# Loading two small inputs of a recurrent layer two tokens per partition, and turning them by products on quarters of the array

## The chip, the core and the metric

The kernel runs on one core of a Trainium2 chip. Its engines each work through a list of instructions of their own: TensorE (PE, matrix products; PEld are its weight loads), VectorE (DVE), ScalarE (ACT), GpSimd (POOL) and SyncE (SP), which here only issues transfers. SBUF is the on-chip memory with 128 partitions, PSUM the memory of 8 banks that TensorE writes, DRAM the memory outside. The metric is the time of one execution on the device in microseconds (us); lower is better.

## The reference

A recurrent attention layer (RWKV-7) over 4 batch elements, 8 heads, 768 tokens and 40 dimensions per head, followed by a feed-forward layer with a squared ReLU:

```python
for t in range(S):
    y[:, :, t] = np.einsum('bhd,bhde->bhe', rt, state)
    Sa = np.einsum('bhde,bhe->bhd', state, at)
    state_decay = state * wt[:, :, None, :] - np.einsum('bhd,bhe->bhde', Sa, bt)
    state = state_decay + np.einsum('bhd,bhe->bhde', vt, kt)
...
x = np.ascontiguousarray(attn_out.transpose(0, 2, 1, 3)).reshape(B * S, H * D)
...
h = np.maximum(x @ w_in, 0.0)
return (h * h @ w_out).astype(np.float32)
```

`r`, `k`, `v`, `w`, `a` and `b` have the shape (4, 8, 768, 40), `w_in` (320, 2048) and `w_out` (2048, 320). What matters for the change: every one of the six inputs has to be brought into SBUF and, but for parts of their use, turned so that the 40 dimensions of a head lie along the partitions and the tokens along the columns.

## The kernel before

The tokens are cut into 24 chunks of 128 tokens of one batch element (`order`). A chunk `i` has an early part, which doesn't depend on the state, and a late part, which does.

The early part (`early`, six steps, written e`i`.1 to e`i`.6 in the order below) loads `w`, `b` and `a` as 128 tokens in 128 partitions by 8 heads of 64 columns, 40 of them used (`fetch`, L146; the buffers are `in_w`, `in_ab` and, for chunks 0 and 1, `in_b`). It turns `w` by four transposes (`turn`, L331), makes the running products of the decays by scans on DVE (L372 to L381, into the tile `decay`, or `dec` for chunks 0 and 1), turns `b` and `a` by four transposes each, multiplies them with the decays (L387, L388), forms products of `a` and `b` within the chunk, and copies them from PSUM into the tile `N` on ScalarE (L401 to L403). Parts of `N` go to DRAM (`kept_q`, `kept_m`, `kept_n`, `kept_d`), and so does the tile of decays (`kept_e`). GpSimd takes the small triangular systems up from there and solves them (L483, L485), in eleven units of 1 to 4 chunks, and stores the result in `kept_t`.

The late part loads `dec` from `kept_e`, `k`, `r`, `v` and `b`, and the solved blocks (`blocks` from `kept_t`, joined to larger inverses by products of 32x32 in `inverses`, tiles `spares`, `T`). It turns `k`, `r` and `v`, and runs `chain`: it begins two banks of `x` from the state, solves for the corrections with `T` and `N` (copies into `apart_x` and `minus_x` on ScalarE in between), updates the state and leaves the tokens of the output in `tokens`. `Ffn` then computes the feed-forward layer on pairs of chunks: `thirds` and `whole` make the hidden units, `square` squares them on ScalarE, and `make_quarter` makes a quarter of the sum over `w_out`. The tokens of a pair are first moved between partitions by eight small transfers (`gather`, L746).

The order of work is written out by hand, in two ways. Up to about 345 us (the opening) it is a list of words: `e3.4` is step 4 of the early part of chunk 3, `LA4` loads `b` and `a` of chunk 4, `lr1` and `lv2` load `r` of chunk 1 and `v` of chunk 2, `sN2` and `sE2` store chunk 2's `N` and decays, `rv1` turns `r` and `v` of chunk 1, `x0` and `c0` are steps of chunk 0's chain, `B1` loads blocks, `J1` joins them, `W1` loads feed-forward weights, `pa` and `pd` round them, `f10` is ten filling products that write nothing of use. An `@a` or `@g` puts a word's transfers on ScalarE's or GpSimd's queue in place of SyncE's. From chunk 7 on it is a fixed slot for each chunk (`sorted_slot`), in which chunk `i` is finished, chunk `i+1` is prepared, and in slots 7 to 13 the early parts of chunks 14 to 23 are done (two each in slots 7 to 9, one each after that). Stores in a slot are put off by one or two places (`store`, `later`, L110). At a slot's end `loads` issues the transfers of the chunk after next.

PSUM is dealt out from three rotating pools: `ps_w` with four banks, `ps_c` with two, `ps_f` with two.

Of the kernel before, what the change touches and what calls it, by code (L numbers as in the profile page):

```python
# [17 lines left out]
def kernel(  # L18
# [73 lines left out]
    def new(name, shape, bufs):  # L92
        return work.tile(shape, FP32, tag=name, name=name, bufs=bufs)
# [37 lines left out]
    for nm, n, fill in (("w", 2, 1.0), ("ab", 4, 0.0), ("b", 2, 0.0)):  # L131
        rings[nm] = Ring(f"in_{nm}", n, [128, H, DP], fill, pads)

# [14 lines left out]

    def load_early(i):
        early_loaded[i] = {nm: fetch(ring, src, i) for nm, ring, src in (("w", "w", w), ("b", "b" if i < 2 else "ab", b), ("a", "ab", a))}  # L150
        if i < 2:
            loaded[i] = {"b": early_loaded[i]["b"]}

# [142 lines left out]
    def as_they_are():  # L296
# [4 lines left out]
        for f in range(NF):  # L301
# [7 lines left out]
    kept_n = [dram.tile([2, HC, NP, HC], FP32, tag=f"n{i}", name=f"kept_n{i}") for i in range(len(order))]  # L309
# [16 lines left out]
                        tag=f"t{u}", name=f"kept_t{u}") for u, (_, nb) in enumerate(units)]  # L326

# [32 lines left out]
    def early(i, g=None, apart=False):  # L360
# [14 lines left out]
        if not apart:  # L375
            bT_, aT_ = turn(x_["b"]), turn(x_["a"])
# [6 lines left out]
        if apart:  # L383
            bT_, aT_ = turn(x_["b"]), turn(x_["a"])
            yield
# [3 lines left out]
        if opened:  # L389
            waiting["e", i] = lambda: on_queue[0].dma_start(out=kept_e[i], in_=dec[:USED])  # L390
        else:
            store(kept_e[i], dec[:USED], 2)
        yield
        bb, c = order[i]
        t_ = new("N", [128, 2, H, HC], 1)


        for e, p_ in enumerate(products(bT, aT[:, :, :C])):
            for group in range(2):
                own_, qs = slice(group * HC, (group + 1) * HC), slice(2 * group, 2 * group + 2)  # L400
                nc.scalar.copy(t_[own_, group, e:NP:2], p_[:HC, qs, :HC])  # L401
                nc.scalar.copy(t_[own_, group, NP + e::2], p_[HC:, qs, HC:])  # L402
            nc.scalar.copy(t_[:HC, 1, e::2], p_[:HC, :, HC:])  # L403
# [14 lines left out]
        if g is None:  # L418
            between = t_[:HC, 1].rearrange("s (w b j) t -> s w b j t", w=2, b=2)
            for e in range(2):  # L420
                moved.append((kept_n[i][e].rearrange("s (w j) t -> s w (j t)", w=2), between[:, :, e].rearrange("s w j t -> s w (j t)"), nc.sync))
# [5 lines left out]
        if g is not None:  # L427
            g["N"] = new("N21", [C, NP, HC], 2)
            for e in range(2):
                nc.scalar.copy(g["N"][e * HC:(e + 1) * HC].rearrange("s (w j) t -> s w j t", w=2),  # L430
                               t_[:HC, 1].rearrange("s (w b j) t -> s w b j t", w=2, b=2)[:, :, e])
            g["joins"] = spare("joins", i)
            for half in range(2):
                nc.scalar.copy(g["joins"][half * HC:half * HC + Q], joins(half))
# [61 lines left out]
    def arrive(i, g, queue=nc.sync):  # L496
        if "N" not in g:
            g["N"] = new("N21", [C, NP, HC], 2)
            queue.dma_start(out=g["N"], in_=kept_n[i].rearrange("b s q t -> (b s) q t"))
# [138 lines left out]
    def chain(i, g):  # L638
# [4 lines left out]
        x_ = [psum(pool)[:, :DM // 2].rearrange("t (h d) -> t h d", d=D) for pool in (ps_w, ps_c)]  # L643
# [266 lines left out]
    fourth = [(n, min(n + 3, NF // 2), flat(t_)) for n, t_ in zip(range(0, NF // 2, 3), rings["ab"].tiles)]  # L910
# [85 lines left out]
    def load_ab(m_):  # L996
        early_loaded.setdefault(m_, {}).update({nm: fetch("ab", src, m_) for nm, src in (("b", b), ("a", a))})
# [87 lines left out]
    def loads(j):  # L1085
        if j < len(order):
            n = ready.setdefault(j, {})
            n["dec"] = kept_here[j % 2]
            nc.sync.dma_start(out=n["dec"][:USED], in_=kept_e[j])
            fetch_next(j, "k", "b")  # L1090
            if not soon(j) and unit_of[j] < FINE:
                arrive(j, n)
            if soon(j) and j > B:
                n["joining"] = inverses(j, n)
                next(n["joining"], None)
# [8 lines left out]
    def sorted_slot(i, g, ch):  # L1104
# [26 lines left out]
        elif more:  # L1131
            begin(j, n)
        step(second.make_quarter)
        if fine and not early_join:
            join()
        step(of(turn_rv), at_place)
        fetch_next(j + 1, "r")
        sums(1)
        step(second.make_quarter, at_place)
        solved_ahead = i > LAID  # L1140
        step(*[on(ch)] * (not solved_ahead), of(decay_state), at_place)
        sums(0)
        sums(2)
# [8 lines left out]
        if not early_join and not fine:  # L1152
            join()
        step(*[on(ch)] * (not solved_ahead), at_place)
        step(at_place, of(turn_k))
        step(of(turn_down), at_place)
        if fine:
            join()
        step(at_place, on(ch))
# [75 lines left out]
```

## Time and profile before

| | |
|---|---|
| time, median of 3 runs (lowest, highest) | 952.38 us (950.92, 957.40) |
| the profiled execution: its time, its span | 956.81 us, 955.1 us |
| mean granted clock of TensorE | 0.945 |
| ScalarE waiting for a turned `r` (L565), in total and longest | 62.8 us, 14.4 us |
| SyncE issues of `in_ab`, median (longest) | 0.67 us (5.98) for `b`, 0.76 us (2.42) for `a` |
| transposes of `in_ab`, from the first to the last | 6.5 to 585.0 us |

The times of rows are microseconds from the start of the span, and the profiled execution is one of several. A group's line in the profile names the engine, the line of the code, the tile written and the tiles read; `128*64 128x80` means 128 rows and 64 columns of weights and 128 by 80 moving elements. A float32 product stands in the trace as two MATMUL rows, a transpose as one. In an order of time, the figure in brackets is how long the engine had been idle and what released it. `SPq` is SyncE's issue of a transfer, `DMA` a transfer that someone waited for.

### The profile page before, as it was taken

The page shows a single profiled execution, that of the slowest core. Times are in us where ns is not written, and L with a number is a line of the kernel's source. Part 1 is how long each engine was busy: PE and PEld are TensorE (multiplying, and loading weights), DVE is VectorE, ACT ScalarE, POOL GpSimd, SP SyncE. Part 2 cuts the span into 40 slices and gives each one's busy share as a digit, 9 for nine tenths or more (in the row PEclk, how much of TensorE's full clock was granted, in tenths as well). Part 3 has the DMA queues.
Part 4 walks back from the last instruction along what each step waited for, and adds up shares of the span by engine and source line. Part 5 has one row for each costly group of instructions (what it writes and reads, how often), then busy time and mean ns, then how long its engine had stood idle before and what let it go on. Part 6 is the DMA issues. An engine that isn't in the chain of part 4 may idle for free.

```text
span 955.1 us, 22646 instructions
## 1 busy us (share of the span) xinstructions
PE 867.8 (91%) x9004; PEld 722.9 (76%) x9004; DVE 444.3 (47%) x1127; ACT 370.0 (39%) x965; POOL 463.0 (48%) x871
## 2 busy tenths in 40 slices
PE   6467888788899999997998999999999999999998
PEld 4345556567777778777787788798899998888897
DVE  5914764888573325543525336443364333333022
ACT  4040535534635254353442553443423333422321
POOL 4557318147003876772059994879999700000000
PEclk9766996878999999998999999999999999999999
DMA  9749858956676567886868644752345443240000
GB/s 106 128 111 146 155 125 164 209 149 121 155 133 143 111 114 160 153 136 125 140 128 133 102 89 80 133 128 49 67 73 93 93 90 66 36 79 1 22 14 14
DMA packets 260338, 102.05 MB, mean 107 GB/s; under 512 B 235594, under 2 KB 249930, under 8 KB 259210
## 3 DMA queue, kind: packets, MB, share of 16 engines
q1 hardware_dynamic: 251493, 83.00, 48.8%
q0 software_dynamic: 3840, 15.79, 6.7%
q10 hardware_dynamic: 4901, 1.83, 0.9%
q8 instruction: 71, 1.16, 0.6%
q14 instruction: 33, 0.27, 0.1%
HBM read 67.82 MB, written 30.79 MB: 103 GB/s over the span
## 4 chain that ended last, share of the span: by engine, by line
PE 67%; DMA 9%; DVE 9%; ACT 7%; SPq 5%; issue 3%; POOL 0%; DVEq 0%; ACTq 0%; POOLq 0%
PE ps_f L87 33%; PE ps_w L87 18%; PE ps_c L87 8%; PE ps_w L331 4%; DMA dec<-kept_e 2%; SPq L110 2%; DMA in_r<-in_r_dram 2%; PE ps_c L691 1%; ACT hid L802 1%; SPq L746 1%; DMA in_w<-in_w_dram 1%; ACT N L402 1%; PE ps_f L264 1%; ACT N L401 1%; PE ps_c L603 1%
## 5 line engine op out<-in xcount | busy, mean ns | idle before, releaser
L485 POOL TENSOR_TENSOR half_t<-half_t,half_p 128x126 f32<-128x126 f32 (+43 forms) x374 | 216.0, 578 | 29.3
L483 POOL TENSOR_TENSOR half_p<-half_n,half_t 128x126 f32<-128x126 f32 (+43 forms) x374 | 196.6, 526 | 63.2 <-DMA half_n<-kept_q 25.8
L87 PE MATMUL ps_f<-tokens,w_in 128*128 128x256 f32 x672 | 157.6, 388 | 0.0
L87 PE MATMUL ps_f<-w_out,hid 128*128 128x160 f32 (+1 forms) x736 | 153.1, 361 | 0.3 <-ACT hid L802 0.3
L87 PEld LDWEIGHTS ps_f<-tokens,w_in 128*128 128x128 f32 x672 | 126.4, 193 | 24.3 <-issue 8.0
L87 PEld LDWEIGHTS ps_f<-w_out,hid 128*128 128x128 f32 x736 | 116.7, 191 | 23.9 <-issue 1.8
L794 ACT ACTIVATE hid<-ps_f 128x512 f32<-128x512 f32 x84 | 49.0, 595 | 110.7 <-PE ps_f L87 109.9
L401 ACT COPY N<-ps_w 64x128 f32<-64x128 f32 x96 | 24.8, 258 | 104.4 <-PE ps_w L87 88.3
L723 DVE TENSOR_TENSOR state<-ps_w,state 40x160 f32<-40x160 f32 x40 | 12.9, 321 | 98.0 <-PE ps_w L87 97.7
L456 POOL DMA_DIRECT2D half_n<-kept_q x20 | 10.5, 529 | 95.9 <-DMA kept_m<-N 32.0
L802 ACT ACTIVATE hid<-hid 128x512 f32<-128x512 f32 x96 | 56.3, 625 | 0.5
L347 DVE TENSOR_TENSOR RX<-ps_w,upper 128x512 f32<-128x512 f32 x48 | 30.9, 685 | 50.1 <-PE ps_w L87 50.1
L372 DVE TENSOR_TENSOR_SCAN decay<-ps_w,ones 128x64 f32<-128x64 f32 x88 | 23.7, 270 | 65.0 <-PE ps_w L331 65.0
L264 PE MATMUL ps_f<-ident 128*128 128x512 f32 (+3 forms) x108 | 50.5, 603 | 0.0
L87 PE MATMUL ps_f<-tokens,w_third 64*128 64x256 f32 x336 | 46.7, 390 | 0.1
L739 DVE TENSOR_TENSOR tokens<-ps_c,dec 128x512 f32<-128x512 f32 x24 | 16.6, 692 | 62.4 <-PE ps_c L87 61.1
L347 DVE TENSOR_TENSOR RV<-ps_w,upper 128x512 f32<-128x512 f32 x48 | 30.9, 684 | 23.9 <-PE ps_w L87 23.6
L565 ACT COPY rT<-ps_w 128x512 f32<-128x512 f32 x24 | 14.1, 586 | 62.9 <-PE ps_w L331 62.8
L331 PE MATMUL ps_w<-ident,in_ab 128*128 128x128 f32 x184 | 26.3, 288 | 10.9 <-DVE RV L347 9.9
L553 DVE TENSOR_TENSOR kvT<-ps_w,dec 128x512 f32<-128x512 f32 x24 | 16.4, 684 | 42.7 <-PE ps_w L331 37.2
L264 PEld LDWEIGHTS ps_f<-ident 128*128 128x128 f32 x108 | 21.2, 214 | 18.9 <-issue 18.0
L87 PE MATMUL ps_w<-rT,kvT 40*128 40x128 f32 x384 | 30.5, 302 | 4.9 <-ACT kvT L566 4.9
(177 smaller groups left out, 1631.5 us busy)
## 6 DMA issues: line engine op xcount, KB each, us to landing
dec<-kept_e SPq DMA_DIRECT2D x22, 633.8 KB
kept_e<-decay SPq DMA_DIRECT2D x19, 633.8 KB
in_w<-in_w_dram SPq DMA_DIRECT2D x24, 160.0 KB
in_b<-in_b_dram SPq DMA_DIRECT2D x24, 160.0 KB
in_ab<-in_a_dram SPq DMA_DIRECT2D x24, 160.0 KB
in_r<-in_r_dram SPq DMA_DIRECT2D x24, 160.0 KB
in_v<-in_v_dram SPq DMA_DIRECT2D x24, 160.0 KB
half_n<-kept_q POOLq DMA_DIRECT2D x14, 256.0 KB, 4.9
```

What stands on the lines that cost most here:

```text
L87: nc.tensor.matmul(o, l_, r_, start=start, stop=True, skip_group_check=True)
L110: later(lambda: queue.dma_start(out=out_, in_=in_), steps)
L264: nc.tensor.matmul(fill_bank[:, :n * 128], ident, ident.unsqueeze(1).to_broadcast([128, n, 128]), start=True, stop=True, skip_group_check= ...
L331: nc.tensor.transpose(p_[:, q * 128:(q + 1) * 128], pair(x_, q), ident)
L347: nc.vector.tensor_tensor(t_, p_, over4(upper), Alu.mult)
L372: nc.vector.tensor_tensor_scan(up[:, q, MID + 1:C + 1], wT[:, q, MID:], ones, 1.0, Alu.mult, Alu.mult)
L401: nc.scalar.copy(t_[own_, group, e:NP:2], p_[:HC, qs, :HC])
L483: eng.tensor_tensor(p_, part[:, at:at + m_].unsqueeze(1).to_broadcast([128, n, m_]), t3[:, :n, s:s + 1].to_broadcast([128, n, m_]), Alu.mult)
L485: eng.tensor_tensor(t3[:, :n, s + 1:], t3[:, :n, s + 1:], p_, Alu.subtract)
L739: nc.vector.tensor_tensor(t_, y_, g["up"][:, :, :C], Alu.mult)
L794: nc.scalar.activation(h_, p_.rearrange("p f t -> p (f t)"), Act.Relu)
L802: nc.scalar.activation(h_, h_, Act.Square)
```

## The change

1. `b` and `a` of the early part come together in one tile `in_ab` of 128 partitions by 8 heads by 128 columns: `b` in partitions 0 to 63, `a` in 64 to 127, each partition with two neighbouring tokens of 40 numbers, so that a row of a transfer has 320 bytes in place of 160. There are two such tiles in place of four smaller ones. Chunks 0 and 1 still have `b` in `in_b`, and only `a` in the new way.
2. `turn_ab` turns them: for each pair of heads, each of the two tokens, each head of the pair and each of `b` and `a` there is one product of a 64x64 part with a 64x64 part of the identity, written to every second column of a half of a bank.
3. `kept_n` is stored by one transfer in place of two, with another order of the columns of `N` (L403 and the copies for chunks 0 and 1 follow that order).
4. The stores of `kept_e` for chunks 14 to 23 are issued by ScalarE in place of SyncE.
5. The first bank of `x` comes from `ps_c` for chunks 0 to 7.
6. In the opening, `lr1` stands directly ahead of `sN2` instead of behind `lv2`.
7. In the slots, `v` is loaded together with `r`, the first step of `inverses` is always done in `loads` for chunks 9 to 15, and the first `square` of a slot comes two steps earlier, behind `turn_down`.
8. The weights' fourth sum, which uses the space of `in_ab`, is laid out for the larger tiles.

```diff
+    rings["ab"] = Ring("in_ab", 2, [128, H, 2 * DP], 0.0, lambda t_: t_[:, :, 2 * D:])
...
+    def fetch_ab(i):
+        bb, c = order[i]
+        t_ = rings["ab"].next()
+        for half, src in enumerate((b, a)):
+            if half or i >= 2:
+                on_queue[0].dma_start(out=t_[half * DP:(half + 1) * DP, :, :2 * D],
+                                      in_=src[bb, :, c * C:(c + 1) * C, :].rearrange("h (p j) d -> p h (j d)", j=2))
+        return t_
...
-    kept_n = [dram.tile([2, HC, NP, HC], FP32, tag=f"n{i}", name=f"kept_n{i}") for i in range(len(order))]
+    kept_n = [dram.tile([2, HC, NP * HC], FP32, tag=f"n{i}", name=f"kept_n{i}") for i in range(len(order))]
...
+    def turn_ab(i, x_):
+
+        banks = [psum(ps_w) for _ in range(2)]
+        t_, b_ = x_["ab"], x_.get("b")
+        if i < 2:
+            for q in range(NP):
+                nc.tensor.transpose(banks[0][:, q * 128:(q + 1) * 128], pair(b_, q), ident)
+        for q in range(NP):
+            for j in range(2):
+                for e in range(2):
+                    for half, p_ in enumerate(banks):
+                        if half or i >= 2:
+                            rows = slice(half * DP, (half + 1) * DP)
+                            mm(p_[e * DP:(e + 1) * DP, q * 128 + j:(q + 1) * 128:2], t_[rows, 2 * q + e, j * D:j * D + DP], ident[rows, rows], q == 0 and j == 0)
+        return [quads(p_) for p_ in banks]
...
-            bT_, aT_ = turn(x_["b"]), turn(x_["a"])
+            bT_, aT_ = turn_ab(i, x_)
...
-            store(kept_e[i], dec[:USED], 2)
+            store(kept_e[i], dec[:USED], 2, nc.scalar)
...
-            for e in range(2):
-                moved.append((kept_n[i][e].rearrange("s (w j) t -> s w (j t)", w=2), between[:, :, e].rearrange("s w j t -> s w (j t)"), nc.sync))
+            moved.append((kept_n[i].rearrange("b s x -> s b x"), t_[:HC, 1].rearrange("s (b h) t -> s b (h t)", b=2), nc.sync))
...
-        x_ = [psum(pool)[:, :DM // 2].rearrange("t (h d) -> t h d", d=D) for pool in (ps_w, ps_c)]
+        x_ = [psum(pool)[:, :DM // 2].rearrange("t (h d) -> t h d", d=D) for pool in (ps_c if i <= LAID else ps_w, ps_c)]
...
-            if not soon(j) and unit_of[j] < FINE:
-                arrive(j, n)
-            if soon(j) and j > B:
+            if unit_of[j] < FINE or soon(j) and j > B:
                 n["joining"] = inverses(j, n)
                 next(n["joining"], None)
...
-        fetch_next(j + 1, "r")
+        fetch_next(j + 1, "r", "v")
...
-        step(of(turn_down), at_place)
+        step(of(turn_down), second.square, at_place)
...
-        fetch_next(j + 1, "v")
-        step(of(turn_state), second.square, second.whole, at_place)
+        step(of(turn_state), second.whole, at_place)
```

Three places show how it moves instructions. The first is TensorE in the opening, from the products of chunk 2 (`decay`, `bT`) over step 4 of chunk 3 (`in_ab`) to the first join (`spares`, `blocks`), before:

```order
L87 MATMUL ps_w<-decay_126,bT 128x128 x8
L331 MATMUL ps_w<-ident,in_ab_78 128x128 x4
L331 MATMUL ps_w<-ident,in_ab_79 128x128 x4
L87 MATMUL ps_w<-spares 32x32 x16
L87 MATMUL ps_w<-blocks,spares 32x32 x16
```

and after:

```order
L87 MATMUL ps_w<-decay_122,bT 128x128 x8
L87 MATMUL ps_w<-ident,in_ab_83 64x64 x32
L87 MATMUL ps_w<-spares 32x32 x16
L87 MATMUL ps_w<-blocks,spares 32x32 x16
L87 MATMUL ps_w<-decay_123,bT 128x128 x8
```

The eight transposes have become 32 small products at the same place. The second is SyncE in the opening, from chunk 2's last store of `N` to chunk 4's loads of `b` and `a`, before:

```order
L423 DMA kept_n_150<-N 128x1x128 x2
L390 DMA kept_e_175<-decay_127 104x1560
L423 DMA kept_q<-N 32x8x32 x2
L423 DMA kept_m_200<-N 32x512
L423 DMA kept_q<-N 32x8x32 x2
L423 DMA kept_m_200<-N 32x512
L423 DMA kept_n_151<-N 128x1x128 x2
L146 DMA in_v_114<-in_v_dram 128x8x40
L146 DMA in_r_110<-in_r_dram 128x8x40
L146 DMA in_ab_80<-in_b_dram 128x8x40
L146 DMA in_ab_81<-in_a_dram 128x8x40
```

and after, from chunk 2's store of decays to its last store of `N`:

```order
L419 DMA kept_e_170<-decay_122 104x1560
L148 DMA in_r_106<-in_r_dram 128x8x40
L452 DMA kept_q<-N 32x8x32 x2
L452 DMA kept_m_195<-N 32x512
L452 DMA kept_q<-N 32x8x32 x2
L452 DMA kept_m_195<-N 32x512
L452 DMA kept_n_146<-N 64x2x256
```

The load of `r` has moved ahead of two chunks' stores, and one store of `kept_n` is left of two. The third is ScalarE in slot 10, after the change, with what each row waits for (PE and DVE are those engines, a DMAHW name with a number is one of eight counters on which SyncE's and ScalarE's transfers are counted in turn; a transfer waits for the last one on its own counter):

```order
L822 ACTIVATE hid<-ps_f 128x512 [waits PE_49] x2
L830 ACTIVATE hid<-hid 128x512 [waits Activation_49] x2
L565 COPY spares<-ps_w 32x256 [waits PE_49]
L565 COPY spares<-ps_w 32x256
L721 COPY xnT<-ps_c 128x512 [waits PE_49]
L110 DMA kept_e_188<-decay_122 104x1560 [waits DMAHW2_49,DVE_49]
L431 COPY N<-ps_w 64x2x64 [waits DMAHW3_49,DMAHW1_49,DMAHW6_49,DMAHW0_49,PE_49]
```

and SyncE at the same place, where the last transfer on counter 2 is the first move of the tokens:

```order
L148 DMA in_r_106<-in_r_dram 128x8x40 [waits DMAHW7_49,PE_49]
L148 DMA in_v_108<-in_v_dram 128x8x40 [waits DMAHW0_49]
L110 DMA out_dram<-o 128x320 [waits DMAHW1_49,Activation_49]
L774 DMA tokens<-tokens 24x256 [waits DMAHW2_49]
L774 DMA tokens<-tokens 16x256 [waits DMAHW3_49]
```

Before, the squares (the second row) stood behind the copy of `sd`, further on in the slot, the store of `kept_e` stood in SyncE's list behind the moves of the tokens, and `in_v` stood there behind the stores of `N`.

More of the change, by code (lines that the diff above doesn't have):

```diff
@@ L130 @@
     rings = {}
-    for nm, n, fill in (("w", 2, 1.0), ("ab", 4, 0.0), ("b", 2, 0.0)):
+    for nm, n, fill in (("w", 2, 1.0), ("b", 2, 0.0)):
         rings[nm] = Ring(f"in_{nm}", n, [128, H, DP], fill, pads)
+    rings["ab"] = Ring("in_ab", 2, [128, H, 2 * DP], 0.0, lambda t_: t_[:, :, 2 * D:])
     def more_rings():
@@ L147, in fetch @@
         return t_
+    def fetch_ab(i):
[6 more added lines that the diff above has]
+        return t_
     def load_early(i):
-        early_loaded[i] = {nm: fetch(ring, src, i) for nm, ring, src in (("w", "w", w), ("b", "b" if i < 2 else "ab", b), ("a", "ab", a))}
+        early_loaded[i] = {"w": fetch("w", w, i)}
         if i < 2:
+            early_loaded[i]["b"] = fetch("b", b, i)
             loaded[i] = {"b": early_loaded[i]["b"]}
+        early_loaded[i]["ab"] = fetch_ab(i)
     def load(i, g=None):
@@ L383, in early @@
         if apart:
-            bT_, aT_ = turn(x_["b"]), turn(x_["a"])
+            bT_, aT_ = turn_ab(i, x_)
             yield
@@ L402, in early @@
                 nc.scalar.copy(t_[own_, group, NP + e::2], p_[HC:, qs, HC:])
-            nc.scalar.copy(t_[:HC, 1, e::2], p_[:HC, :, HC:])
+            nc.scalar.copy(t_[:HC, 1].rearrange("s (b w j) t -> s w b j t", w=2, j=2)[:, :, :, e],
+                           p_[:HC, :, HC:].rearrange("s (w b) t -> s w b t", w=2))
         moved = []
@@ L418, in early @@
         if g is None:
-            between = t_[:HC, 1].rearrange("s (w b j) t -> s w b j t", w=2, b=2)
-            for e in range(2):
-                moved.append((kept_n[i][e].rearrange("s (w j) t -> s w (j t)", w=2), between[:, :, e].rearrange("s w j t -> s w (j t)"), nc.sync))
+            moved.append((kept_n[i].rearrange("b s x -> s b x"), t_[:HC, 1].rearrange("s (b h) t -> s b (h t)", b=2), nc.sync))
         if opened:
@@ L429, in early @@
             for e in range(2):
-                nc.scalar.copy(g["N"][e * HC:(e + 1) * HC].rearrange("s (w j) t -> s w j t", w=2),
-                               t_[:HC, 1].rearrange("s (w b j) t -> s w b j t", w=2, b=2)[:, :, e])
+                nc.scalar.copy(g["N"][e * HC:(e + 1) * HC], t_[:HC, 1, e * NP:(e + 1) * NP])
             g["joins"] = spare("joins", i)
@@ L498, in arrive @@
             g["N"] = new("N21", [C, NP, HC], 2)
-            queue.dma_start(out=g["N"], in_=kept_n[i].rearrange("b s q t -> (b s) q t"))
+            queue.dma_start(out=g["N"], in_=kept_n[i].rearrange("b s (q t) -> (b s) q t", q=NP))
             if unit_of[i] < FINE:
@@ L909 @@
     sums = [t_.rearrange("p n q t -> p (n q t)")[:, :NF // 2 * HM].rearrange("p (f c) -> p f c", c=HM) for t_ in decays.tiles]
-    fourth = [(n, min(n + 3, NF // 2), flat(t_)) for n, t_ in zip(range(0, NF // 2, 3), rings["ab"].tiles)]
+    fourth = [(n, min(n + 6, NF // 2), flat(t_)) for n, t_ in zip(range(0, NF // 2, 6), rings["ab"].tiles)]
     lower, upper_w = w_out[:, :NF // 2], w_out[:, NF // 2:]
@@ L996, in load_ab @@
     def load_ab(m_):
-        early_loaded.setdefault(m_, {}).update({nm: fetch("ab", src, m_) for nm, src in (("b", b), ("a", a))})
+        early_loaded.setdefault(m_, {}).update(ab=fetch_ab(m_))
     def advance(u, n_):
```

2 lines of the change are left out of this document (1 added, 1 removed).

## The prediction

> **What bounds the kernel now.** I read the head of the page first, then the table of stages, then the chain that ended last, then the order of time of TensorE, ScalarE and SyncE at the places where the chain leaves TensorE. The head gives the span and the engines; in the table the columns are the stage, its length, busy time with instruction counts, the granted clock, the share of the DMA engines and GB/s.
>
> ```profile
> span 955.1 us, 22646 instructions
> PE 867.8 (91%) x9004; PEld 722.9 (76%) x9004; DVE 444.3 (47%) x1127; ACT 370.0 (39%) x965; POOL 463.0 (48%) x871
> 56.00:110.00 54.00, 36.42 (x334) 27.12 (x334) 20.83 (x49) 18.85 (x52) 31.45 (x82) 0.72 0.83 150
> 110.00:210.00 100.00, 86.13 (x959) 62.62 (x958) 68.57 (x173) 43.68 (x120) 35.19 (x90) 0.81 0.77 160
> 210.00:310.00 100.00, 87.64 (x898) 70.83 (x898) 64.33 (x182) 51.70 (x136) 31.63 (x75) 0.95 0.68 137
> 310.00:420.00 110.00, 106.98 (x1207) 86.89 (x1205) 46.73 (x145) 48.73 (x138) 81.55 (x221) 1.00 0.69 132
> 420.00:500.00 80.00, 73.13 (x823) 61.20 (x824) 30.81 (x93) 35.03 (x100) 27.26 (x63) 0.96 0.78 136
> 500.00:586.00 86.00, 80.64 (x856) 66.37 (x855) 36.72 (x97) 33.42 (x87) 79.61 (x75) 0.98 0.61 104
> 586.00:860.00 274.00, 271.69 (x3072) 243.06 (x3072) 113.66 (x195) 102.29 (x246) 145.12 (x165) 1.00 0.43 82
> ```
>
> There are three regimes. Up to about 110 us TensorE is idle a third of the time at a granted clock of 0.72 while the DMA engines are 83% busy. From 310 us on TensorE is the bound: 97%, 91%, 94% and 99% of the stages. Only 2.3 of 274 us are free after 586, so nothing can be won there. Between lies a mixture. The waits that the change aims at are these; the figure in brackets is TensorE's idle time ahead of the group.
>
> ```profile
> 83.65 1.08 PE L331 MATMUL ps_w<-ident,in_r 128*128 128x128 f32 x4 [6.28 <-DMA in_r<-in_r_dram]
> 439.73 1.07 PE L87 MATMUL ps_w<-spares 32*32 32x32 f32 x32 [4.88 <-DVE kvT L553]
> 478.77 0.69 PE L87 MATMUL ps_w<-spares 32*32 32x32 f32 x32 [0.42 <-DVE kvT L553]
> 505.69 0.95 PE L331 MATMUL ps_w<-ident,in_v 128*128 128x128 f32 x4 [3.57 <-DMA in_v<-in_v_dram]
> ```
>
> The third row is the second one's twin in the next slot: without the wait it idles 0.42 us and takes 0.69 us, after the wait 1.07. A wait of several us also costs some of the clock behind it.
>
> **The price of the quarters.** Before, `b` and `a` of a chunk are 8 transposes of 128x128; now they are 32 products of 64x64 by 64 columns (chunks 0 and 1: 4 transposes and 16 products). The trace has no such product, so I take start to start from its neighbours. A product of the code is two MATMUL rows of the trace, a transpose is one.
>
> ```profile
> 640.56 0.60 PE L331 MATMUL ps_w<-ident,in_r 128*128 128x128 f32 x4
> 641.00 0.60 PE L331 MATMUL ps_w<-ident,in_v 128*128 128x128 f32 x4
> 628.78 0.50 PE L87 MATMUL ps_w<-state,dec 128*64 128x80 f32 x8
> 629.11 0.61 PE L87 MATMUL ps_w<-in_v,A 128*64 128x40 f32 x16
> 629.55 0.48 PE L87 MATMUL ps_c<-state,dec 128*64 128x80 f32 x8
> 622.26 1.06 PE L87 MATMUL ps_w<-dec,kvT 40*128 40x128 f32 x16
> 623.15 1.03 PE L87 MATMUL ps_f<-tokens,w_third 64*128 64x256 f32 x8
> ```
>
> Four transposes take 641.00 - 640.56 = 0.44 us, 110 ns each, 0.88 us a chunk. With 64 columns of weights, 8 products over 40 columns take 629.55 - 629.11 = 0.44, 55 ns each, and 4 over 80 take 0.33, 82 ns each. The new ones, over 64, lie between 55 and 82; I take 60, nearer the lower row, since that one has the same weights, and half of a 128-column product (0.89 / 8 = 111 ns, row 622.26) is 56. A chunk then costs 32 x 60 = 1.92 us, 1.04 more than before.
>
> How much of it is on the path? In the slots of chunks 7 to 13 (about 345 to 586 us), where chunks 14 to 23 are turned, TensorE has no cover: 10 x 1.04 = 10.4. In the opening, chunks 2, 5, 6, 7 and 9 are turned ahead of waits that other engines set:
>
> ```profile
> 45.70 1.08 PE L87 MATMUL ps_w<-in_v,A 128*64 128x40 f32 x16 [2.31 <-DVE decay L381]
> 143.99 1.05 PE L87 MATMUL ps_w<-spares 32*32 32x32 f32 x32 [4.82 <-DVE spares L525]
> 181.72 0.80 PE L87 MATMUL ps_w<-apart_x,T 128*64 128x80 f32 x8 [3.16 <-DVE RV L347]
> 254.74 0.50 PE L87 MATMUL ps_w<-state,dec 128*64 128x80 f32 x8 [1.71 <-ACT T L544]
> ```
>
> These five cost nothing while those waits stand; were all of them gone, 5.2 us would come on top. Chunks 4, 8 and 10 to 13 pay in full and chunk 3 half: 6.5 x 1.04 = 6.8. Chunks 0 and 1 lie under DVE's scans and the solve. **Term: +17** (from +1 if two quarters ran at once, 0.08 us a chunk, to +29 at 82 ns).
>
> **The earlier load of r.** The chain has 14.5 us of one transfer:
>
> ```profile
> 48.34 0.39 SPq L390 DMA_DIRECT2D kept_e<-decay  x1
> 69.00 14.51 DMA in_r<-in_r_dram
> ```
>
> Now it is issued right behind the kept_e store of row 48.34, some 20 us sooner; its buffer is free since r of chunk 0 was turned. TensorE's 6.28 us go, and products that ran slow behind them get a little faster. But chunk 4's `b` and `a`, issued right behind, and the weights behind them are late next, with the DMA at 83%. **Term: -6** (-9 to 0).
>
> **Half the packets.** The early `b` and `a` come in rows of 320 instead of 160 bytes: 46 transfers of 160 KB, 1024 packets each, become 512 each.
>
> ```profile
> in_ab<-in_a_dram SPq DMA_DIRECT2D x24, 160.0 KB
> in_ab<-in_b_dram SPq DMA_DIRECT2D x22, 160.0 KB
> q1 hardware_dynamic: 251493, 83.00, 48.8%
> q0 software_dynamic: 3840, 15.79, 6.7%
> ```
>
> Queue 1 averages 330 bytes and 0.488 x 16 x 955.1 us / 251493 = 29.7 ns a packet, queue 0 4112 bytes and 267 ns. The line through both gives 19 ns at 160 and 29 at 320 bytes. So 46 x (1024 x 19 - 512 x 29) ns = 212 us of 16 engines, 13 us each, are saved, an estimate. Three quarters of it lie where TensorE or DVE sets the pace. **Term: -3** (-8 to 0). The Trainium skill, "DMA: Bandwidth & Descriptors", section "Specifications", speaks against it: below 512 bytes a transfer does not reach line rate, and 320 is below too. By that this term would be nothing and the sum 954; the line through the two queues says only that small packets are dearer per byte.
>
> **Stores and ScalarE.** One kept_n store a chunk instead of two saves a DMA issue of about 0.6 us each on SyncE, once on ScalarE and once on POOL. Most have cover: **-1** (-2 to 0). Ten kept_e stores move into ScalarE's order. Each waits for DVE's last product and, as the order with waits shows, for one earlier SyncE transfer: the load of k behind chunks 15, 17 and 19, the first move of the tokens in chunks 16 and 20. Behind it are queued the N copies or the copies of r and v, for which TensorE waits.
>
> ```profile
> 419.33 7.82 DMA dec<-kept_e
> 420.49 0.37 SPq L146 DMA_DIRECT2D in_k<-in_k_dram  x1
> 424.51 0.59 ACT L565 COPY rT<-ps_w 128x512 f32<-128x512 f32 x1
> 480.28 0.59 ACT L693 COPY xnT<-ps_c 128x512 f32<-128x512 f32 x1
> 484.81 0.26 ACT L401 COPY N<-ps_w 64x128 f32<-64x128 f32 x1 [3.94 <-PE ps_w L87]
> 486.73 9.01 SPq L746 DMA_DIRECT2D tokens<-tokens  x8
> ```
>
> k is issued behind a transfer that lands at 427.15, so r's copy could start 2.6 us late. In slot 10 ScalarE is free for its store at 480.87, but the tokens leave at 486.73; with some 2 us to land, the N copies start near 488.5 instead of 484.81. TensorE has 3.6 us of other work there. I take **+1.5** (0 to +6), since SyncE will be somewhat less late.
>
> **The two waits in the slots.**
>
> ```profile
> 435.67 2.90 DMA blocks<-kept_t
> 438.66 0.45 DVE L525 STREAM_TRANSPOSE spares<-blocks 128x256 f32<-128x256 f32 x1 [6.60 <-DMA blocks<-kept_t]
> 502.35 3.20 DMA in_v<-in_v_dram
> ```
>
> At 438.66 DVE waits 6.6 us for the blocks of chunk 10, issued last in SyncE's queue, and k's product stands behind that in DVE's order. Now they are issued with the loads at the end of the slot before, ahead of the stores: 4.88 us and about 0.8 of slow clock go, **-5.5** (-6 to -2). Late next there is dec, just in time at 427.15. v of chunk 12 is now issued right behind r, over 20 us earlier: **-3** of 3.57 (-4 to 0), since dec for the same slot then becomes the latest.
>
> **Squares and banks.** The squares leave the stretch ahead of the copies of `apart_x` for a pause of ScalarE. These copies hold TensorE up for 3.4 us in the whole kernel:
>
> ```profile
> L87 PE MATMUL ps_w<-apart_x,T 128*64 128x80 f32 x384 | 24.7, 253 | 10.7 <-DVE RV L347 4.5 <-ACT apart_x L656 3.4 <-ACT hid L275 2.7
> ```
>
> **-1.5** (-2.5 to +1). The first x bank of chunks 0 to 7 comes from ps_c instead of ps_w; both pools wait for copies that are long done: nothing (-1 to +1).
>
> **Sum:** +17 - 6 - 3 - 1 + 1.5 - 5.5 - 3 - 1.5 = -1.5 us. Against the profiled execution's 956.8 that is 955.3; that execution lay 4.4 us above the median of the runs, 952.4, so I predict 951.
>
> **Rivals.** *Dear quarters* (slower): if a 64x64 product that writes every second column takes as long as the rows with 80 columns, 82 ns, the first term is +29 and the time 963; at the 111 ns of a full product it would be 978. It decides from about 80 ns on. For it speaks that no row writes with a stride; against it that the rows follow the number of columns.
>
> *Two quarters at once* (faster): the products alternate between halves of the rows and write two banks. If halves overlapped, each would count 30 ns, the first term would shrink to +1 and the time be 935. Row 622.26 speaks against: it alternates between halves of the rows and between two banks, and takes 111 ns a product, no less than a full one. The Trainium skill, "TensorEngine Tiling (Array Packing)", section "Key Properties", says that different tiles run in parallel; the trace does not show it.
>
> *Transfers are the real bound of the opening* (faster): the 38 us from 69 to 107 are bound by the DMA, and r and the packets give 9 and 8 us instead of 6 and 3, with the kept_n stores 2 and the slots another 2: 939. The 0.83 share speaks for it, TensorE's 86 to 97% behind 110 us against.
>
> *ScalarE held up* (slower): if SyncE is as late in four slots as at 486.73, each costs about 2.5 us in place of 1.5 altogether, and the time is 960. *Packets as dear as their bytes* (the change doesn't do what it says): 954.
>
> **How the numbers follow.** A measurement of this kernel tells about 1% from no change, 9.5 us. My forecast has 0.46, packets that bring nothing 0.12, quarters at once 0.10, transfers as the bound 0.11, dear quarters 0.15, ScalarE held up 0.06. The two faster cases make 0.21. Dear quarters and most of the last one (with another term on its bad side) make 0.21 slower, the rest is 0.58. The forecast's own range, from its terms' nearer ends, is 944 to 959. For 8 in 10 the range reaches into both outer cases, 936 to 966, and leaves out the cheapest quarters and full-price ones.
>
> **What would show it.** Right: some 32 products on `in_ab` per chunk with starts 1.9 us over all; no wait for `in_r` near 84, for the blocks near 440 or for `in_v` near 505; TensorE still above 95% from 310 us on. Wrong: quarter groups of 1 us or of over 2.6 us; ScalarE idle ahead of N copies with a transfer as releaser in slots 8 to 10; opening and slots moving by more than 10 us in one direction.

## The result, and the profile after

The changed kernel takes 940.88 us (median of 4 runs, 938.07 to 942.44), the kernel before in the same comparison 953.5 us (4 runs, 950.92 to 957.4): ratio 0.986, 95% interval 0.982 to 0.990. It is 1.4% faster. A second comparison, with 6 and 11 runs, gave 940.77 against 955.14 us, ratio 0.986 (0.982 to 0.989). The forecast was 951 us, within 1% of before. The time lies in the range of 936 to 966, in its lower third, but below the forecast's own narrower range of 944 to 959, and the gain is clear of noise. The profiled execution after took 938.07 us, before 956.81, so these two stand 18.7 us apart where the medians stand 12.6 apart: what is read from the pair of traces is read as mechanism and place, and sizes come from the medians. A part of the gain goes with the clock: among all runs at a mean granted clock of 0.952 to 0.954, four of the changed kernel took 940.3 to 942.4 us and six of the kernel before 946.9 to 949.8, some 7 us apart. The rest of the 12.6 stands beside a higher clock of the changed kernel, 0.956 against 0.945 in the profiled executions; no run separates the two.

The head of the page after and its queues, then the table of stages (columns as before: stage, length, busy time with instruction counts, granted clock, DMA share, GB/s):

```profile
span 936.3 us, 25166 instructions
...
PE 872.9 (93%) x10292; PEld 726.5 (78%) x10292; DVE 446.4 (48%) x1126; ACT 370.2 (40%) x965; POOL 463.2 (49%) x868
...
q1 hardware_dynamic: 223891, 76.51, 44.4%
```

```profile
56.00:110.00 54.00, 41.67 (x472) 29.61 (x472) 26.70 (x65) 20.83 (x59) 33.51 (x83) 0.81 0.82 165
...
420.00:500.00 80.00, 76.46 (x1092) 62.90 (x1091) 34.82 (x104) 35.20 (x95) 37.53 (x64) 1.00 0.75 141
500.00:586.00 86.00, 85.17 (x1154) 71.08 (x1153) 36.41 (x84) 40.40 (x111) 69.07 (x64) 1.00 0.53 101
586.00:860.00 274.00, 271.35 (x2927) 243.47 (x2927) 111.60 (x187) 95.47 (x226) 137.73 (x158) 1.00 0.39 73
```

TensorE does 5 us more work in a span 19 us shorter. The stage from 56 us has 41.7 us of it in place of 36.4, at a clock of 0.81 in place of 0.72; the two stages of the slots are full (96% and 99%) at a clock of 1.00. After 586 us TensorE is as full as before. (The stages are the same stretches of time in both tables; the changed kernel is further on in its work.) The three places at which the forecast expected waits to go, and the quarters themselves, in the order of time of TensorE after:

```profile
77.91 1.23 PE L87 MATMUL ps_w<-rT,kvT 40*128 40x128 f32 x16 [0.73 <-ACT kvT L594]
...
82.68 0.33 PE L87 MATMUL ps_w<-ident,in_ab 64*64 64x64 f32 x2
84.24 1.16 PE L87 MATMUL ps_w<-ident,in_ab 64*64 64x64 f32 x62 [1.23 <-issue]
...
95.66 1.07 PE L87 MATMUL ps_w<-spares 32*32 32x32 f32 x32 [3.02 <-DVE spares L553]
...
385.08 1.16 PE L87 MATMUL ps_w<-ident,in_ab 64*64 64x64 f32 x64
386.18 0.66 PE L360 MATMUL ps_w<-ident,in_k 128*128 128x128 f32 x4
...
425.04 0.69 PE L87 MATMUL ps_w<-spares 32*32 32x32 f32 x32 [0.42 <-DVE kvT L581]
...
487.60 0.60 PE L360 MATMUL ps_w<-ident,in_v 128*128 128x128 f32 x4
```

No wait for `r` is left (6.28 us before), the join has 0.42 in place of 4.88 us, and `in_v` none in place of 3.57. Two waits are left in the opening. Within the turn of chunk 4's `b` and `a` TensorE stops for 1.23 us; the row behind the stop is the first product that reads `a`. And the join of chunk 1 waits 3.02 us, where it waited 2.29 us before already:

```profile
104.26 0.69 PE L87 MATMUL ps_w<-spares 32*32 32x32 f32 x32 [2.29 <-DVE spares L525]
```

A chunk's 32 quarter products take 386.18 - 385.08 = 1.10 us from start to start, where 1.92 was forecast and the eight transposes took 0.88.

### The profile page after: what moved, and what is told of

It is laid out like the page before. It is cut to its first block, busy times and chain, and to the rows that moved or that the text cites. A ratio compares the mean times of both kernels' runs of the same rounds, so it can differ in the third digit from the quotient of the medians.

```text
span 936.3 us, 25166 instructions
## 1 busy us (share of the span) xinstructions
PE 872.9 (93%) x10292; PEld 726.5 (78%) x10292; DVE 446.4 (48%) x1126; ACT 370.2 (40%) x965; POOL 463.2 (49%) x868
## 4 chain that ended last, share of the span: by engine, by line
PE 74%; DVE 11%; ACT 6%; DMA 4%; issue 2%; SPq 2%; ACTq 0%; POOL 0%; DVEq 0%; POOLq 0%
PE ps_f L87 37%; PE ps_w L87 20%; PE ps_c L87 8%; PE ps_w L360 4%; PE ps_f L277 2%; DMA blocks<-kept_t 2%; PE ps_c L631 1%; PE ps_c L719 1%; ACT N L432 1%; DVE decay L410 1%; DMA in_ab<-in_b_dram 1%; DVE decay L409 1%; ACT N L431 1%; DVE half_t L511 1%; DVE half_t L513 1%
## 5 line engine op out<-in xcount | busy, mean ns | idle before, releaser
L511 POOL TENSOR_TENSOR half_p<-half_n,half_t 128x126 f32<-128x126 f32 (+43 forms) x374 | 200.4, 536 | 66.4 <-DMA half_n<-kept_q 29.9
L513 POOL TENSOR_TENSOR half_t<-half_t,half_p 128x126 f32<-128x126 f32 (+43 forms) x374 | 212.9, 569 | 29.3
L87 PE MATMUL ps_w<-ident,in_ab 64*64 64x64 f32 x1472 | 32.9, 233 | 12.7 <-DVE RV L376 9.2
L87 PEld LDWEIGHTS ps_w<-ident,in_ab 64*64 64x64 f32 x1472 | 28.7, 146 | 20.1 <-DVE RV L376 9.8
L581 DVE TENSOR_TENSOR kvT<-ps_w,dec 128x512 f32<-128x512 f32 x24 | 16.5, 686 | 48.2 <-PE ps_w L360 41.8
```

Of the source, the lines that this page charges most:

```text
L87: nc.tensor.matmul(o, l_, r_, start=start, stop=True, skip_group_check=True)
L511: eng.tensor_tensor(p_, part[:, at:at + m_].unsqueeze(1).to_broadcast([128, n, m_]), t3[:, :n, s:s + 1].to_broadcast([128, n, m_]), Alu.mult)
L513: eng.tensor_tensor(t3[:, :n, s + 1:], t3[:, :n, s + 1:], p_, Alu.subtract)
L581: nc.vector.tensor_tensor(kT, kT_, down[:, :, 1:C + 1], Alu.mult)
```

## The experiments

Three sets were run. The first takes the change apart, the second asks how TensorE executes a quarter, the third what the loads and the stores on ScalarE do. "Before" in each line is the kernel before on the same chip.

### The parts of the change, each alone

The kernel before with one word moved:

```diff
-e2.6 sE2 sN2 J0 e3.3 ... lv2 lr1 S1.20
+e2.6 sE2 lr1 sN2 J0 e3.3 ... lv2 S1.20
```

> The kernel before with one word moved: r of chunk 1 is loaded directly ahead of chunk 2's stores of N; nothing else is changed. Theory 1 (the opening's gain is the wait for r): TensorE's wait of 6.3 us at 83.65 goes, everything behind it comes 5 to 9 us sooner up to the slots, and the time is 945 to 949. Theory 2 (the gain is the halved packets, which let the blocks and the next loads land sooner): r lands sooner, but TensorE waits at the blocks or at the loads of chunk 4 instead; less than 3 us are won, 950 to 953.

Measured: 944.42 us against 951.62, ratio 0.993 (0.990 to 0.995), as theory 1 says, and a little better than its range. In its order of time the two later waits are still there, the first of them smaller without having been touched:

```profile
429.96 0.69 PE L87 MATMUL ps_w<-spares 32*32 32x32 f32 x32 [2.14 <-DVE kvT L553]
...
495.37 0.98 PE L331 MATMUL ps_w<-ident,in_v 128*128 128x128 f32 x4 [3.53 <-DMA in_v<-in_v_dram]
```

The kernel before with the moves in the slots (point 7 of the change):

```diff
-        fetch_next(j + 1, "r")
+        fetch_next(j + 1, "r", "v")
...
-            if not soon(j) and unit_of[j] < FINE:
-                arrive(j, n)
-            if soon(j) and j > B:
+            if unit_of[j] < FINE or soon(j) and j > B:
...
-        step(of(turn_down), at_place)
+        step(of(turn_down), second.square, at_place)
```

> The kernel before with the three moves in the slots alone: v loaded with r, blocks of a chunk issued with the loads of the slot before, the first square two steps earlier. Theory 1: the gap of 4.9 us before the join at 439.73 and that of 3.6 us before in_v at 505.69 go; time 944 to 947, TensorE busy over 76 of 80 us in slots 9 and 10. Theory 2 (the loads of b and a in 160-byte rows keep SyncE and the DMA late): dec or k is late in their place, and 948 to 953 is left.

Measured: 946.77 us against 951.62, ratio 0.996 (0.994 to 0.998): theory 1 holds for the join and `in_v`, and theory 2 for what comes behind. `dec` is late next, as the prediction had said: DVE waits 4.27 us for its load, and DVE's scans of the decays, which stand behind that, hold TensorE up.

```profile
493.83 0.60 PE L331 MATMUL ps_w<-ident,in_v 128*128 128x128 f32 x4
...
500.74 0.73 DVE L575 TENSOR_TENSOR f<-end,dec 128x4 f32<-128x4 f32 x1 [4.27 <-DMA dec<-kept_e]
...
506.41 1.12 PE L587 MATMUL ps_w<-ident,dec 128*128 128x128 f32 x4 [1.50 <-DVE decay L381]
```

The kernel before with points 1, 2 and 8 alone, the two-token loading and the quarters:

> The kernel before with b and a in two tokens a partition and turned by quarters; stores, slots, order of words and banks as before. Theory 1 (two quarters run at a time, 29 ns each, so turning costs about 0.2 us a chunk more than the transposes; the halved packets bring little): 950 to 955, TensorE still waits for r near 84 us. Theory 2 (the halved packets are the opening's gain): r lands 5 us sooner or more, and the time is 943 to 948.

Measured: 944.75 us against 951.62, ratio 0.994 (0.991 to 0.997). The expectation of 950 to 955 was wrong, though it had the quarters at the right price. Without any of the moves, all three waits are gone:

```profile
78.20 0.60 PE L360 MATMUL ps_w<-ident,in_r 128*128 128x128 f32 x4
...
432.78 0.69 PE L87 MATMUL ps_w<-spares 32*32 32x32 f32 x32 [0.42 <-DVE kvT L582]
...
494.30 0.60 PE L360 MATMUL ps_w<-ident,in_v 128*128 128x128 f32 x4
```

Its page has for queue 1, with 46 x 512 packets fewer than before and the same bytes:

```profile
q1 hardware_dynamic: 227941, 83.00, 46.2%
```

So the three parts win 7.2, 4.9 and 6.9 us alone, 19 in sum, and about 13 together. They work on the same waits. What is left when one part is taken out of the whole shows it too, here the changed kernel with the old loads, their four tiles and the transposes:

```diff
...
-            bT_, aT_ = turn_ab(i, x_)
+            bT_, aT_ = turn(x_["b"]), turn(x_["a"])
...
```

> The changed kernel with b and a loaded in 160-byte rows into four tiles and turned by transposes as before; all else of the change stays. Theory 1: the time stays within 3 us of the changed kernel, 938 to 943, as the quarters and the packets are both worth little. Theory 2: most of the gain goes, 946 to 952.

Measured: 938.09 us against 951.62, ratio 0.986 (0.982 to 0.990), the ratio of the whole change, as theory 1 says. Beside the moves, the two-token loading brings nothing.

### How TensorE executes a quarter

The changed kernel with the order of the quarter products alone changed, twice. First all of `b`, then all of `a`:

```diff
+        for half, p_ in enumerate(banks):
...
+                for q in range(NP):
+                    for j in range(2):
+                        for e in range(2):
```

And in runs, one quarter eight times, then the next:

```diff
+        for e in range(2):
+            for half, p_ in enumerate(banks):
...
+                    for q in range(NP):
+                        for j in range(2):
```

> The changed kernel with the 32 quarter products of a chunk in another order: first the 16 of b (rows 0 to 63 of the tile), then the 16 of a (rows 64 to 127), with the two halves of the columns still in turn. Theory A (two neighbours run together when they read different halves of the rows): nothing overlaps now but the one pair in the middle, a product counts 55 to 60 ns, a chunk's group 1.8 to 1.95 us in place of 1.1, and the time is 9 to 14 us above the changed kernel. Theory B (any two different quarters run together, those of two halves of the columns too): 1.1 us and the time unchanged. Theory C (one quarter takes 29 ns, and nothing overlaps): 1.1 us and the time unchanged.

> The changed kernel with the quarter products in runs of eight that use the same quarter of the array. Theories A and B: a product counts 55 to 60 ns, 1.75 to 1.95 us a chunk, 9 to 14 us on the whole time. Theory C: 1.1 us.

Measured: 949.65 us (ratio 0.9998, 0.997 to 1.002, all of the gain gone) and 981.37 us (one run). A chunk's group, from its start to the next group's, with halves apart and then with runs:

```profile
374.68 1.91 PE L87 MATMUL ps_w<-ident,in_ab 64*64 64x64 f32 x64
376.52 0.81 PE L87 MATMUL ps_f<-w_out,hid 128*128 128x320 f32 x2
```

```profile
371.30 3.40 PE L87 MATMUL ps_w<-ident,in_ab 64*64 64x64 f32 x64
374.63 0.55 PE L360 MATMUL ps_w<-ident,in_k 128*128 128x128 f32 x3
```

From start to start the first is 376.52 - 374.68 = 1.84 us, which is what theory A gave; the second is 374.63 - 371.30 = 3.33 us, out of reach of all three theories. Theory A falls with it: if a product counted 58 ns alone, runs of one quarter would take 1.86 us too. The starts of the single MATMUL rows say what happens. In runs they come 58 ns apart one by one, so that a product, which has two rows, takes 116 ns. With halves apart they come in pairs 6 to 7 ns apart, a pair every 58 ns. In the changed kernel they come in fours, a four every 58 ns. A product is two passes of 58 ns on its quarter, and passes of different quarters run side by side: two of them with the halves apart (the two halves of the columns), four in the changed kernel. That became theory D and was put to the test with two more changes in one kernel. Only two quarters come in turn, the two halves of the rows at one half of the columns, or (odd chunks) two diagonal ones:

```diff
+        for e_ in range(2):
+            for q in range(NP):
+                for j in range(2):
+                    for half, p_ in enumerate(banks):
...
+                            e = (e_ + half * (i % 2)) % 2
```

And the products for `A` take one half of the rows, then the other:

```diff
+            for e in range(2):
+                for q in range(NP):
+                    rows = slice(e * DP, e * DP + D)
+                    mm(ps[e][:, q], l_[rows, q, :], r_[rows, q, :], True)
```

> The changed kernel with less alternation at two places. (1) The quarter products of a chunk use only two quarters in turn: in even chunks the two halves of the rows at one half of the columns, in odd chunks two diagonal quarters. (2) The eight products of kvT with dec that make A (rows dec,kvT) go through one half of the rows first and then the other, in place of alternating. Theory D: a float32 product is two passes, one row of the trace each, of about 58 ns for 64 moving columns and 111 ns for 128, and passes of up to four different quarters run side by side. Then a chunk's quarter group takes 1.8 to 1.95 us in both kinds of chunks, and the group of A 1.75 to 1.9 us in place of 1.06; the time is 20 to 35 us above the changed kernel's. Rival 1 (the prediction's reading of the row of dec and kvT: halves of the rows do not overlap at 128 columns of weights): the group of A stays at 1.0 to 1.1 us. Rival 2 (row halves overlap only where the column half is the same): 1.85 us in even chunks and 3.3 us in odd ones.

Measured: 964.65 us, one run, 24 above the changed kernel on the same chip. In the order of time, the quarters of an even chunk, the products of `A` (and of the group behind it, `tokens`), the quarters of an odd and of an even chunk:

```profile
360.34 1.91 PE L87 MATMUL ps_w<-ident,in_ab 64*64 64x64 f32 x64
...
367.14 1.27 PE L87 MATMUL ps_w<-dec,kvT 40*128 40x128 f32 x13
368.15 0.48 PE L87 MATMUL ps_f<-tokens,w_third 64*128 64x256 f32 x1
368.25 0.38 PE L87 MATMUL ps_w<-dec,kvT 40*128 40x128 f32 x2
368.47 0.38 PE L87 MATMUL ps_f<-tokens,w_third 64*128 64x256 f32 x1
368.48 0.27 PE L87 MATMUL ps_w<-dec,kvT 40*128 40x128 f32 x1
...
383.04 1.91 PE L87 MATMUL ps_w<-ident,in_ab 64*64 64x64 f32 x64
...
399.75 1.91 PE L87 MATMUL ps_w<-ident,in_ab 64*64 64x64 f32 x64
```

The quarters take as long as with the halves apart, 1.84 us from start to start: any two quarters, neighbours in rows or diagonal, run together, and rival 2 falls. The sixteen passes of A now start over 368.48 - 367.14 = 1.34 us, and with the last pass of 0.11 take 1.45 us, where they took 0.89 when the halves alternated: rival 1 falls. That is less than the 1.75 to 1.9 that theory D forecast, because the two halves still meet: at the seam, three passes start only 4 to 6 ns behind another (so there are 13 starts, 111 ns apart, for 16 passes), and the next group's products begin between the last of A's, as the rows at 368.15 and 368.47 show.

A kernel in which the two halves of the rows write one bank was not run.

### The loads, and the stores on ScalarE

Why does the two-token loading take away waits that it doesn't touch? Two kernels leave out half of each early transfer of `b` and `a`, so half of its packets and of its bytes, and are otherwise the kernel before, zeros standing in the tiles for what is not loaded. In the one, half of the heads:

```diff
+        hs = slice(0, NP if ring == "ab" else H)
+        on_queue[0].dma_start(out=t_[:, hs, :D], in_=src[bb, hs, c * C:(c + 1) * C, :].rearrange("h t d -> t h d"))
```

In the other, half of the tokens:

```diff
+        n = HC if ring == "ab" else C
+        on_queue[0].dma_start(out=t_[:n, :, :D], in_=src[bb, :, c * C:c * C + n, :].rearrange("h t d -> t h d"))
```

> The kernel before, but the early b (from chunk 2 on) and a are loaded for four of the eight heads only, and zeros stand for the others: instructions, issues, their order and the transposes stay, and each of these 46 transfers has 512 packets of 160 bytes in place of 1024. Theory P (the time of the DMA engines in packets is what made r, the blocks and v late): TensorE's waits at 83.65, 439.73 and 505.69 of before shrink under 1.5 us each without any of the moves, and the time is 941 to 947. Theory Q (something else of the two-token layout did it: fewer buffers, the turning's place or length): the waits stay, 949 to 953.

> The kernel before, but the early b (from chunk 2 on) and a are loaded for the first 64 of a chunk's 128 tokens only, zeros for the others: 512 packets of 160 bytes to 64 partitions a transfer, where the run with half of the heads had 512 packets to 128 partitions. Theory E (r was held up in the opening by the transfers of b and a spread over all 128 partitions; those to 64 partitions leave it a part of the DMA engines): TensorE's wait for r near 84 us shrinks under 2 us, as with two tokens a partition, and the time is 940 to 945. Rival (it is not the partitions): the wait stays at 5 to 7 us, and the time is 941 to 946.

Measured: 943.51 us against 951.05 (ratio 0.992, 0.989 to 0.994) and 942.52 against 955.14 (0.989, 0.984 to 0.994). The order of time of the first, and behind it of the second:

```profile
84.85 1.09 PE L335 MATMUL ps_w<-ident,in_r 128*128 128x128 f32 x4 [5.92 <-DMA in_r<-in_r_dram]
...
437.35 0.69 PE L87 MATMUL ps_w<-spares 32*32 32x32 f32 x32 [0.41 <-DVE kvT L557]
...
497.51 0.60 PE L335 MATMUL ps_w<-ident,in_v 128*128 128x128 f32 x4
```

```profile
84.39 1.09 PE L335 MATMUL ps_w<-ident,in_r 128*128 128x128 f32 x4 [6.29 <-DMA in_r<-in_r_dram]
...
431.71 0.69 PE L87 MATMUL ps_w<-spares 32*32 32x32 f32 x32 [0.42 <-DVE kvT L557]
...
491.92 0.60 PE L335 MATMUL ps_w<-ident,in_v 128*128 128x128 f32 x4
```

Theory P holds in the slots: with half the packets (and bytes) the join and `v` are in time. It fails in the opening, and theory E with it: `r` is as late as before. So neither half the packets nor 64 partitions in place of 128 explain why `r` was in time with two tokens a partition. The traces show another difference there, in SyncE's issue of `r` and GpSimd's first issues of seven loads, with half of the heads and then with two tokens a partition:

```profile
70.24 0.61 SPq L150 DMA_DIRECT2D in_r<-in_r_dram  x1
69.63 1.05 POOL L460 DMA_DIRECT2D half_n<-kept_q  x2 [12.29 <-DMA kept_q<-N]
```

```profile
70.14 0.60 SPq L148 DMA_DIRECT2D in_r<-in_r_dram  x1
70.85 1.05 POOL L485 DMA_DIRECT2D half_n<-kept_q  x2 [11.99 <-DMA kept_n<-N]
```

GpSimd's loads go through queue 0, whose packets take 74% of the DMA engines' time from 70.5 to 78 us in the first of these traces and 58% in the second. In the kernel before and in the three runs in which `r` is late, GpSimd begins 0.6 us ahead of the issue of `r`; with two tokens a partition it begins 0.7 us behind it. So `r` seems to have been in time because it got ahead of these loads; no run tests this alone, and what put GpSimd back stays open.

The stores of `kept_e` were put back on SyncE, in the changed kernel and in the one with the old loads:

```diff
-            store(kept_e[i], dec[:USED], 2, nc.scalar)
+            store(kept_e[i], dec[:USED], 2)
```

> The changed kernel with the stores of kept_e for chunks 14 to 23 issued by SyncE again. Theory H (the store holds ScalarE up in slot 10 behind the transfer of the tokens): the wait of 7 us of ScalarE ahead of the N copies near 471 goes, TensorE no longer waits for sd and apart_x near 476, and 1 to 3 us are won, 937 to 940. Rival: SyncE, with ten issues more, brings r, v, dec or the blocks late in a slot, a new wait of TensorE of 1 us or more stands there, and the time is the changed kernel's or up to 4 us more.

> The changed kernel with b and a in 160-byte rows turned by transposes as before, and with the stores of kept_e on SyncE as before: of the change stay the moves of r, v, blocks and squares, one store of kept_n and the banks. Theory 1 (the moves alone take all the waits, and the wait of 3.6 us for sd near 474 is the store on ScalarE): that wait goes, 933 to 937, faster than the changed kernel. Rival: with all of the packets back and ten issues more, SyncE is late in a slot and the time is 938 to 943.

> The changed kernel once more, beside the run without its two-token loading on the same chip. Expected 938 to 942; the difference to that run is what the two-token loading is worth beside the moves, by theory 1 of the first runs within 3 us of nothing.

What they take away is seen in ScalarE's and SyncE's order of the changed kernel in slot 10:

```profile
463.90 0.58 ACT L721 COPY xnT<-ps_c 128x512 f32<-128x512 f32 x1
470.99 0.31 ACTq L110 DMA_DIRECT2D kept_e<-decay  x1
471.49 0.26 ACT L431 COPY N<-ps_w 64x128 f32<-64x128 f32 x1 [7.01 <-DMA tokens<-tokens]
```

```profile
461.78 7.01 SPq L110 DMA_DIRECT2D out_dram<-o  x1
468.84 8.22 SPq L774 DMA_DIRECT2D tokens<-tokens  x8
```

ScalarE is free at 464.48 and has its store next; the store waits for the first move of the tokens, which SyncE issues at 468.84; so the N copies start at 471.49. With the old loads the same place is worse, and TensorE pays for it; with the stores on SyncE that wait is gone. These are the kernel with the old loads and stores on ScalarE, and the changed kernel with stores on SyncE:

```profile
469.62 0.26 ACT L402 COPY N<-ps_w 64x128 f32<-64x128 f32 x1 [8.85 <-DMA tokens<-tokens]
...
473.75 0.80 PE L87 MATMUL ps_c<-state,dec 128*64 128x80 f32 x8 [3.57 <-ACT sd L604]
```

```profile
469.94 0.26 ACT L431 COPY N<-ps_w 64x128 f32<-64x128 f32 x1 [3.90 <-PE ps_w L87]
...
472.25 0.32 PE L87 MATMUL ps_w<-blocks,spares 32*32 32x32 f32 x9 [1.86 <-issue]
```

Measured for the changed kernel with stores on SyncE: 938.65 us against 951.05, ratio 0.987 (0.982 to 0.991). Theory H names the wait rightly: ScalarE's wait is gone, and with it 0.48 and 0.52 us in which TensorE waited for `sd` and `apart_x`. But no gain can be told from the changed kernel's 0.986: a wait of 1.86 us inside a join, for nothing that the profile shows (1.06 in the changed kernel), stands there, which belongs to neither expectation.

With the old loads and the stores on SyncE: 934.97 us (932.42 to 937.03) against 955.14, ratio 0.980 (0.977 to 0.984), as theory 1 says. On the same chip the changed kernel took 940.77 (937.41 to 941.66). The expected difference of at most 3 us between the two was missed: it is 5.8, and the two kernels differ in the stores too. So the moves, without the two-token loading and without the stores on ScalarE, beat both kernels: 2.0% faster than before, and by medians 5.8 us ahead of the whole change, with no overlap of the single runs.

## Why the prediction was right and where it failed

- **The quarters, +17: wrong, and this is the step that made the forecast "no change".** That the time still lies in the range is owed to the range's width and not to this term. 60 ns a product came from rows with 64 columns of weights, and the rival of overlapping quarters was argued down with row 622.26: "takes 111 ns a product, no less than a full one". The "full one" was a transpose, which is one pass. A full product is two passes of 111 ns (so they come when one half of the rows has TensorE to itself), 222 ns, and row 622.26 has 16 of them in 0.89 us, 56 ns a pass: its halves did run side by side, as the run that took their alternation away shows (1.45 us). The rows from which 60 ns was taken have two halves of the columns in turn, so that they too were prices of an overlap, of two; the quarters overlap by four. A chunk's group measured 1.10 us, 0.22 over the transposes, so the term should have been 16.5 x 0.22 = +3.6. The forecast's own sum would then have been -14.9 and the time 937.5, against 940.9 measured. The run with the halves apart checks the rest of the sum: there a product does cost 58 ns, near the 60 of the forecast, and the kernel took 949.65 us, near the 951. The rival *Two quarters at once* (935) had the right mechanism, with four in place of two. The Trainium skill, "TensorEngine Tiling (Array Packing)", section "Key Properties", which says that different tiles can run in parallel, agrees with the traces; the prediction said that the trace did not show it, and it did.
- **r, -6: right.** Alone it gave 7.2 us, TensorE's wait went, and chunk 4's `a` became late, as the text had said: TensorE stops ahead of its first use for 1.05 us in that run and 1.23 after the whole change, and for nothing before. The chunk-10 join then also had a shorter wait, 2.14 us.
- **Packets, -3: mis-sized, and not a term of its own.** The prices of a packet were nearly right: in the traces' packet records a packet of 160 bytes took 21 ns in the mean before (forecast 19), one of 320 bytes 29 with the two-token loading alone and 26 in the changed kernel (forecast 29). But queue 1 spent 0.488 x 16 x 955.1 = 7457 us before and 0.462 x 16 x 942.7 = 6968 with the two-token loading alone, 31 us less on each engine in place of 13. At 21 and 29 ns the packets that were saved make 19 of them; the other packets became a little cheaper too (the remaining ones of 160 bytes took 20 ns). Alone the loading won 6.9 us, after it had paid for the quarters, since all three waits were gone (that for `r` perhaps by the order of two issues, as shown above); beside the moves nothing was left to win. The rival *Packets as dear as their bytes* falls, and with it, for these sizes, what the prediction drew from the Trainium skill's "DMA: Bandwidth & Descriptors", "Specifications": 320 bytes cost 29 ns, not twice 21.
- **The two gaps in the slots, -5.5 and -3, and the squares, -1.5: right in place.** Both waits go, and the two stages are full at a clock of 1.00. Before, TensorE ran at a granted clock of 0.50 from 439.7 to 443 us, right behind the first wait, and of 0.51 from 505.9 to 509.3, right behind the second. Alone these moves gave 4.9 us of the 10, since `dec` was late next, as the text had said, and TensorE then waited 1.50 us for the decays behind it.
- **ScalarE held up, +1.5: the mechanism is right.** The trace shows it as described, in slot 10 only. Its price depends on the rest: none that can be measured beside the quarters (0.986 against 0.987), perhaps 0.6% with the old loads (0.986 against 0.980, on two chips; the intervals overlap a little, so this isn't settled).
- **The moves together.** r, kept_n, gaps and squares were forecast at -6 -1 -5.5 -3 -1.5 = -17; the kernel with these and the banks alone came out at a ratio of 0.980, 19 us. The sum of the moves was good, though the parts do not add up when they are made alone; the error lies in the price of the quarters.
- *Transfers are the real bound of the opening* (939) gave a time near the measured one, but not the place: behind the opening the slots gained as well. Of *ScalarE held up* (960) one slot in place of four is true. *Dear quarters* (963) would have come with less alternation (949.65 and 981.37 in the two runs), not because of the columns, as it had said.

## What to carry to other kernels

Before a price is taken from a row, count its passes and ask what ran beside it: a time per product is worth something only with the order in which the parts of the array came. Products on quarters are cheap when four different quarters come in turn, three times as dear in runs of one. And several remedies for lateness of the same queue are not to be added: each was worth 5 to 7 us alone, and the two-token loading nothing beside the other two.

## What was not expected of the hardware

- Passes start out of strict order. At the seam between two runs that use different parts of the array, a pass of the later run starts 4 to 6 ns behind one of the earlier run which still has passes to do (three pairs in A's sixteen passes), and rows of the next group stand between the last rows of a group.
- A float32 product of 64 columns on one quarter takes 116 ns when nothing runs beside it, and 29 ns of TensorE's time when three others do.
- In six traces of kernels with quarters, TensorE stopped once in slot 10 inside a join, for 0.55 to 1.86 us, with nothing that the profile shows as the cause; in those with transposes, and in the run that also takes the passes of `A` apart, no such stop is seen. In all six a packet of 16 KB on queue 8, the one that the profile calls `instruction`, ends 1.4 to 1.7 us before TensorE goes on. That TensorE waited for its instructions is therefore a reading to test; the cause is open.
